# Local attention and two mixture layers on one core: six weight tiles issued from GpSimd, shared TensorE tile shapes, and a new order of passes

## The chip, the cores and the metric

One core of a Trainium2 chip runs the whole program. The metric is the device time of one execution in microseconds (us); the median of three executions of the kernel before is 485.14 us.

## What is computed

Attention over q, k and v of shape (2, 8, 576, 64) makes x; two layers follow, each a product with a 512 x 2048 matrix, a function of each element, and a product with a 2048 x 512 matrix.

```python
def _attn_ref(q, k, v):
    # q_d, k_d, v_d: means over groups of 4 positions
    out_d = sm_attn(q_d, k_d, v_d)              # coarse attention, 144 positions
    out_up = np.repeat(out_d, factor, axis=2)
    mask = np.abs(pos[:, None] - pos[None, :]) < factor
    scores = scale * np.matmul(q, k.transpose(0, 1, 3, 2))
    scores = np.where(mask, scores, -1000000000.0)
    ...
    return (out_up + out_local).astype(np.float32)

def _moe_ref(x, w_in, w_out, a, b):
    h = x @ w_in
    P = a[0] + a[1] * h + a[2] * h2 + a[3] * h3
    Q = 1.0 + np.abs(b[0]) * np.abs(h) + np.abs(b[1]) * h2
    g = P / (Q + 1e-06)
    return (g @ w_out).astype(np.float32)

def _moe2_ref(x, w_in, w_out):
    h = x @ w_in
    g = h * np.tanh(np.log1p(np.exp(h)))        # h itself where h > 20
    return (g @ w_out).astype(np.float32)
```

The weights arrive as 64-bit floats, the rest as 32-bit floats.

## The kernel before, in words

**Attention** is cut into 18 units. A unit (function `unit`) takes two heads and 256 positions (two of the 18, called mixed here, take the last 64 positions of all eight heads). Its steps are: load q (line 635); transpose it on TensorE (`flip`, line 537); write the mask into PSUM by a product with two identity matrices (line 694, `eye2` and `mask`, 64 partitions); add the local scores of 48 keys per 32 positions (line 701, output tiles of 32 columns of the array); make the coarse scores of 144 keys (line 707, one product per head, output tiles of 64 columns); softmax on VectorE, ScalarE and GpSimd (lines 719 to 762); transpose the probabilities (lines 773 and 778); multiply by v (lines 803 and 813); write the result in two parts, `xh` (rounded) and `xl` (the rest, line 857 on GpSimd). Eight times, function `prep` loads k, transposes it, copies it on ScalarE (line 578), sums groups of four on VectorE (line 588) and scales the sums (line 591).

**Weights** come in 32 tiles of 1 MB. Each is loaded by SyncE (lines 968 and 973) into one of two buffers `raw`, turned from 64-bit to 32-bit on ScalarE (lines 985 and 992) and VectorE (line 999, which frees the `raw` buffer), and split into a rounded part (line 1011) and a rest (line 1016), which together are a tile `wi` or `wo`.

**Layers.** A step of the first layer multiplies x by two column blocks of `w_in` (line 1129), reads the product from PSUM in three passes (ScalarE: square, line 1149, and absolute value, line 1152; VectorE: line 1158), forms the quotient, and multiplies by `w_out` (line 1262). From the second group of columns on, the quotient uses a logarithm and a sigmoid (lines 1084 and 1089), each with its table load (line 1073). The second layer has its own products (lines 1443, 1499 and 1264).

**Order.** No instruction is placed by hand. Class `Plan` keeps tasks with an engine, an estimated duration, a priority (smaller is earlier) and dependencies, plays them through in time, and writes each engine's instructions in the order in which they come up. Where it sees TensorE without work while little was done in the last 3.4 us, it puts in a product of zeros (line 519, called a filler here) that nothing reads. The order that results is fixed in the program: each engine works through its own list and waits where an operand is late.

Of the kernel before, what the change touches and what calls it, by code (L numbers as in the profile page):

```python
# [72 lines left out]
class Task:  # L73
    __slots__ = ("engs", "fn", "prio", "deps", "out", "next", "take", "use", "started", "ended", "seq", "dens", "port", "dma", "sub")


class Plan:
# [6 lines left out]
    def add(self, engs, fn, prio, after=(), take=(), use=(), chain=None, dens=0.5, port=False, dma=(), sub=None):  # L84
        t = Task()
        t.dma, t.sub = dma, sub
# [24 lines left out]
    def run(self, names):  # L111
# [3 lines left out]
        landed, moved = [0.0] * QUEUED, 0.0  # L115
# [75 lines left out]
        while True:  # L191
            for e in names:
# [3 lines left out]
                while ready[e]:  # L196
# [14 lines left out]
                    if e == "pool" or e == "dve" and t.port:  # L211

                        begin = max(now, port[0])
                        port[0] = begin + t.engs[e]
                    end = until[e] = begin + t.engs[e] * (2 if e == "pe" and now < COLD else 1)
                    there = end + LAT[e]
                    if t.dma:
                        end = begin
# [4 lines left out]
                        until[e], there = end, landed[-1]  # L223
# [25 lines left out]
            while events and events[0][0] <= now + 1e-9:  # L249
# [5 lines left out]
                if kind == 2:  # L255
                    del live[t.slot.space][id(t)]
                    continue
# [12 lines left out]
def kernel(  # L270
# [34 lines left out]
    eye2 = const.tile([64, 128], BF16, name="eye2")  # L305
    mask = const.tile([64, 11, WK], BF16, name="mask")
# [162 lines left out]
    def eyes():  # L469
        for h in range(2):  # L470
            nc.vector.tensor_copy(out=eye2[:, 64 * h:64 * h + 64], in_=ident[:64, :64])
# [10 lines left out]
    t_id = add({"pool": 1.1}, lambda: make_identity(nc, ident), -1000)  # L482
    t_m = add({"dve": 0.1}, lambda: nc.vector.memset(band, 0.0), -1900)
    t_cd = add({"dve": 0.6}, zeros, -1000)
# [48 lines left out]
    SCALE = 0.125  # L533
# [5 lines left out]
    def prep(bb, p, prio, slots, start):  # L539
# [36 lines left out]
        def copy(e, dst, src):  # L576
            if e == "act":
                nc.scalar.activation(out=dst(), in_=src(), func=AF.Identity)
            else:
                nc.vector.tensor_copy(out=dst(), in_=src())  # L580
# [6 lines left out]
        def red():  # L587
# [3 lines left out]
            nc.vector.tensor_scalar(out=kd[p], in0=kd[p], scalar1=SCALE / 16.0, scalar2=None, op0=ALU.mult)  # L591

        kv_done[p] = add({"dve": 0.67 + t_dve(SD, True)}, red, prio, after=copies)
# [27 lines left out]
    def unit(u, slots, start):  # L621
# [42 lines left out]
        def qcopy(e):  # L664
            dst, src = qT.v[:, :256], qp.v[:, :256]
            if e == "act":
                nc.scalar.activation(out=dst, in_=src, func=AF.Identity, scale=SCALE)
# [891 lines left out]
```

## Time and profile before

| what | value |
|---|---|
| median of three executions | 485.14 us (484.02 to 485.44) |
| the profiled execution | 484.05 us |
| its span | 482.3 us |
| TensorE clock granted | 1.00 throughout |
| TensorE, VectorE, ScalarE, GpSimd busy | 98%, 79%, 71%, 12% of the span |
| fillers in the program | 74 |

The profiled execution is 1.75 us longer than its span, which is time ahead of the first and behind the last instruction. The busy share of TensorE counts fillers as work, and the ends of its instructions are modelled; what one step costs is read from the start of one instruction to the start of the next.

### The profile page before, as it was taken

Reading aid. Unit: us, or ns where it says so; the run is one execution under the profiler, and the core shown is the slowest. Engines: PE = TensorE matmul, PEld = TensorE weight load, DVE = VectorE, ACT = ScalarE, POOL = GpSimd, SP = SyncE. Lnnn points to the kernel's source line nnn. Section 1 sums busy time; section 2 is a strip of 40 time slices with the busy share of each in tenths; the row PEclk is TensorE's granted clock in tenths of the full one; section 3 lists DMA queues with packets and bytes.
Section 4 is the critical chain, followed back from the end, with each engine's and each line's share of the span. In section 5 each row is a group of like instructions: output and inputs, shape, how many; then the busy total and the mean of one; then the engine's idle time right before and its main releaser. Section 6 shows DMA issues by size and latency. Waiting matters only on the chain.

```text
span 482.3 us, 9623 instructions
## 1 busy us (share of the span) xinstructions
PE 472.1 (98%) x3944; PEld 429.2 (89%) x3944; DVE 381.1 (79%) x569; ACT 340.6 (71%) x531; POOL 58.0 (12%) x80
## 2 busy tenths in 40 slices
PE   9989999999999999999989999999999999999996
PEld 5667788889999999999989999999989898989885
DVE  5768999989999988978999999678586769624342
ACT  5768887986889898996899987569666446422320
POOL 2664246752000000000000000000000000000000
PEclk9999999999999999999999999999999999999999
DMA  8878779620432224340412001224304220000103
GB/s 181 199 163 200 189 188 246 167 57 18 170 99 79 87 88 174 96 166 1 137 39 88 1 12 76 87 58 165 121 16 167 87 88 1 1 0 1 65 1 130
DMA packets 45980, 47.16 MB, mean 98 GB/s; under 512 B 30576, under 2 KB 31344, under 8 KB 45936
## 3 DMA queue, kind: packets, MB, share of 16 engines
q1 hardware_dynamic: 45936, 46.54, 33.9%
q8 instruction: 31, 0.51, 0.5%
q14 instruction: 13, 0.11, 0.1%
HBM read 44.17 MB, written 2.36 MB: 96 GB/s over the span
## 4 chain that ended last, share of the span: by engine, by line
PE 85%; DVE 4%; ACT 4%; DMA 4%; SPq 2%; issue 1%; POOL 0%; ACTq 0%; POOLq 0%
PE psum L1264 20%; PE psum L1262 20%; PE psum L1129 18%; PE psum L1443 12%; PE psum L1499 7%; DMA att<-in_q_dram 4%; PE psum L519 2%; PE psum L537 1%; PE psum L813 1%; PE psum L803 1%; PE psum L707 1%; PE psum L701 1%; SPq L650 1%; DVE wo L1016 1%; ACT L1073 1%
## 5 line engine op out<-in xcount | busy, mean ns | idle before, releaser
L1129 PE MATMUL psum<-xh,wi 128*128 128x384 f32 (+1 forms) x336 | 82.4, 318 | 2.0 <-ACT late_f L1152 1.8
L1262 PE MATMUL psum<-gg,wo 128*128 128x384 f32 (+1 forms) x480 | 75.9, 312 | 0.0
L1262 PEld LDWEIGHTS psum<-gg,wo 128*128 128x128 f32 x480 | 72.7, 189 | 0.6 <-issue 0.5
L1129 PEld LDWEIGHTS psum<-xh,wi 128*128 128x128 f32 x336 | 58.7, 189 | 3.7 <-ACT late_f L1152 2.1
L1129 PE MATMUL psum<-xl,wi 128*128 128x384 f32 (+1 forms) x168 | 52.4, 312 | 0.0
L1264 PE MATMUL psum<-wo,gg 128*128 128x512 f32 x216 | 51.7, 391 | 0.0
L1264 PE MATMUL psum<-wo,late_g 128*128 128x512 f32 x216 | 51.3, 391 | 0.0
L1264 PEld LDWEIGHTS psum<-wo,late_g 128*128 128x128 f32 x216 | 40.4, 188 | 8.0
L1264 PEld LDWEIGHTS psum<-wo,gg 128*128 128x128 f32 x216 | 40.4, 188 | 8.0
L999 DVE SCALAR_TENSOR_TENSOR wt<-wt,raw 128x1024 int32<-128x1024 int32 x32 | 39.8, 1248 | 6.8 <-ACT wt L985 6.6
L985 ACT ACTIVATE wt<-raw 128x1024 f32<-128x1024 f32 x32 | 36.6, 1142 | 8.1 <-DVE wo L1016 3.5
L992 ACT ACTIVATE raw<-raw 128x1024 int32<-128x1024 uint16 x32 | 36.6, 1146 | 3.9 <-DMA raw<-in_moe_w_out_dram 2.5
L1499 PE MATMUL psum<-xh,wi 128*128 128x384 f32 x128 | 34.4, 335 | 0.0
L1129 PEld LDWEIGHTS psum<-xl,wi 128*128 128x128 f32 x168 | 31.8, 189 | 0.0
L1375 DVE TENSOR_TENSOR part<-psum,part 128x512 f32<-128x512 f32 x27 | 17.8, 687 | 13.7 <-PE psum L1264 13.7
L1149 ACT ACTIVATE wrk<-psum 128x768 f32<-128x768 f32 (+1 forms) x27 | 19.8, 735 | 8.3 <-PE psum L1129 8.0
L1129 PE MATMUL psum<-xh,late_r 128*128 128x384 f32 x96 | 25.3, 334 | 0.0
L1016 DVE TENSOR_TENSOR wo<-wt,wo 128x1024 fp32r<-128x1024 f32 x14 | 17.8, 1274 | 9.4 <-ACT wo L1011 9.4
L1011 ACT ACTIVATE wo<-wt 128x1024 fp32r<-128x1024 f32 x13 | 13.8, 1061 | 16.0 <-DVE wt L1005 7.6
L1499 PEld LDWEIGHTS psum<-xh,wi 128*128 128x128 f32 x128 | 23.3, 188 | 0.2
L1073 ACT ACT_TABLE_LOAD x17 | 21.8, 1283 | 0.3
L1499 PE MATMUL psum<-xl,wi 128*128 128x384 f32 x64 | 21.4, 335 | 0.0
(164 smaller groups left out, 1044.0 us busy)
## 6 DMA issues: line engine op xcount, KB each, us to landing
raw<-in_moe_w_in_dram SPq DMA_DIRECT2D x16, 1024.0 KB, 5.3
raw<-in_moe_w_out_dram SPq DMA_DIRECT2D x16, 1024.0 KB, 5.0
att<-in_v_dram SPq DMA_DIRECT2D x64, 48.0 KB, 2.7
out_dram<-part SPq DMA_DIRECT2D x9, 256.0 KB, 2.1
att<-in_q_dram SPq DMA_DIRECT2D x16, 128.0 KB, 6.4
att<-in_k_dram SPq DMA_DIRECT2D x6, 288.0 KB, 5.3
att<-in_v_dram SPq DMA_DIRECT2D x6, 256.0 KB, 5.9
wrk<-in_k_dram SPq DMA_DIRECT2D x2, 288.0 KB
```

Of the source, the lines that this page charges most:

```text
L985: nc.scalar.activation(out=t.v, in_=words(r)[:, :, 1].bitcast(F32), func=AF.Prelu if fold else AF.Identity, scale=2.0 ** -112, **({"alpha" ...
L992: nc.scalar.activation(out=words(r)[:, :, 0], in_=r.v.bitcast(U16).rearrange("p (n four) -> p n four", four=4)[:, :, 1], func=AF.Copy, sca ...
L999: nc.vector.scalar_tensor_tensor(out=ti, in0=ti, scalar=3, in1=words(r)[:, :, 0], op0=ALU.logical_shift_left, op1=ALU.bitwise_or)
L1016: ENG[e].tensor_tensor(out=w.v[:, 1], in0=s.v, in1=w.v[:, 0].bitcast(F32), op=ALU.subtract)
L1073: nc.scalar.preload_act_table_set(name)
L1129: nc.tensor.matmul(st.h.v[:, i, :T], w.v[:, ww, ks], xx[:, kk, c0:c0 + T], start=(nn == 0 and (st.big or i == 0)), stop=(nn == 3 * KD - 1 ...
L1149: nc.scalar.activation(out=vw(st.a), in_=H(), func=AF.Square)
L1262: nc.tensor.matmul(A(d)[:, :T], w.v[:, ww, lo + d * 128:lo + (d + 1) * 128], vw(gg)[:, i, :], start=start, stop=stop)
L1264: nc.tensor.matmul(A(d), vw(gg)[:, i, sl], w.v[:, ww, lo:lo + DM], start=start, stop=stop)
L1375: nc.vector.tensor_tensor(out=pv, in0=acc.v[:, j], in1=pv, op=ALU.add)
L1443: nc.tensor.matmul(dst.v[:, :TW], wv.v[:, ww, at:at + 128], x(h, kk), start=bool(take) and nn == 0, stop=nn == 5, skip_group_check=not take,)
L1499: nc.tensor.matmul(h.v[:, i, :TW], w.v[:, ww, at:at + 128], xx[:, kk, c0:c0 + TW], start=nn == 0, stop=nn == 3 * KD - 1)
```

## The change

The six weight tiles that are needed first are issued by GpSimd, on a DMA queue of its own, and no longer by SyncE between the attention's loads. The mask product now has 128 partitions (the lower 64 are zeros), and the coarse scores are made in two pieces of 32 rows per head, in the same 64x32 tiles of the array that the local scores use. The scale of the scores moves: k is copied with 0.125/16, q with 16, so the separate scaling of the summed k is gone. The planner's model of DMA becomes one of queues that share the engines, and its priorities change: offsets per unit and per weight tile, and 15 less for the three passes that read a step's product.

```diff
-SECOND = 2.0
+SECOND = 1.6
-LEAD, CLEAD, LLEAD, OLAG = 38, 14, 40, 18
-PROL, PSTEP, VOFF, VROFF, LOFF, KOFF = -45, 3.0, 1, -1, 7, 12
+LEAD, CLEAD, LLEAD, OLAG = 38, 20, 25, 20
+PROL, PSTEP, VOFF, VROFF, LOFF, KOFF = -45, 2.5, 1, -1, 7, 12
-SUMS = 10
+SUMS = 15
+APART, PISSUE = 6, 1.2
+UOFF = [0.0, 0.0, 0.0, 0.0, 3.0, 3.0, 3.0, 3.0, 10.5, 6.0, 6.0, -1.5, 1.5, 3.0, 10.5, -4.5, 4.5, -7.5]
+GOFF = [-8.0, 0.0, 0.0, 0.0, -4.0, 0.0, -8.0, -2.0, -6.0, -4.0, 2.0, 4.0]
+HP = 15
...
+class Rings:
...
+            heads = [r[0] for r in rows.values() if r]
+            live = [j for j in heads if j[0] <= at + 1e-9]
...
+                j[1] -= (to - at) / len(live)
...
-                            end = max(end, landed[-QUEUED]) + issue
-                            moved = max(moved, end + 0.3) + move
-                            landed.append(moved + LAT["sp"])
+                            if len(lane) >= QUEUED:
+                                end = max(end, lane[-QUEUED].done + LAT["sp"])
+                            end += issue
+                            lane.append(Job())
+                            rings.put(now, e, end + 0.3, move, lane[-1])
...
-    eye2 = const.tile([64, 128], BF16, name="eye2")
-    mask = const.tile([64, 11, WK], BF16, name="mask")
+    eye2 = const.tile([128, 128], BF16, name="eye2")
+    mask = const.tile([128, 11, WK], BF16, name="mask")
...
+    def under():
+        nc.vector.memset(eye2[64:], 0.0)
+        nc.vector.memset(mask[64:], 0.0)
...
+    KSCALE = 0.125 / 16.0
+    QSCALE = 16.0
...
-                nc.scalar.activation(out=dst(), in_=src(), func=AF.Identity)
+                nc.scalar.activation(out=dst(), in_=src(), func=AF.Identity, scale=KSCALE)
...
-            nc.vector.tensor_scalar(out=kd[p], in0=kd[p], scalar1=SCALE / 16.0, scalar2=None, op0=ALU.mult)
...
-                    nc.tensor.matmul(sd2()[h], qds(i)[h], kd[p][h], start=(i == 0), stop=(p == pairs[-1]))
+                    for r0 in (h.start, h.start + HB):
+                        c0 = r0 - h.start
+                        nc.tensor.matmul(
+                            sd2()[r0:r0 + HB], qds(i)[h, c0:c0 + HB], kd[p][h], start=(i == 0), stop=(p == pairs[-1]),
+                            tile_position=(h.start, r0),
+                        )
...
-        def load(g=g, r=r):
+        def load(g=g, r=r, q=nc.gpsimd if len(W) < APART else nc.sync):
...
-        x = add({"sp": 0.5}, load, pr - LLEAD, take=[r], chain="wld", dma=[(0.5, 3.97)])
+        x = add({"pool" if len(W) < APART else "sp": 1.0}, load, pr - LLEAD, take=[r], chain="wld", dma=[(PISSUE if len(W) < APART else 0.5, 3.97)])
...
-        ta = add({"act": t_act(n, True)}, i_a, pr, after=th, take=[st.a], use=[st.h], chain="ia")
-        tb = add({"act": t_act(n, True, 1)}, i_b, pr, after=th + [t_b], take=[st.b], use=[st.h], chain="ib")
+        ta = add({"act": t_act(n, True)}, i_a, pr - HP, after=th, take=[st.a], use=[st.h], chain="ia")
+        tb = add({"act": t_act(n, True, 1)}, i_b, pr - HP, after=th + [t_b], take=[st.b], use=[st.h], chain="ib")
...
-        t1 = add({"dve": t_dve(n, ptr=1)}, d_1, pr, after=[ta, t_b], take=[st.c], use=[st.a, st.h], chain="ic")
+        t1 = add({"dve": t_dve(n, ptr=1)}, d_1, pr - HP, after=[ta, t_b], take=[st.c], use=[st.a, st.h], chain="ic")
```

In the program that comes out, lines after the first few hundred have numbers about 50 to 60 higher. Three places are shown.

GpSimd, from the mask's bands (`band`) to the first normalisation of a softmax, before:

```order
L449 AFFINE_SELECT band<-band 64x92
L452 AFFINE_SELECT band<-band 64x92
L474 MEMSET bias_69 128x1
L475 MEMSET bias_69 128x1
L607 TENSOR_TENSOR att<-att 72x4x128
L611 TENSOR_TENSOR att<-att 72x2x2x64
L757 TENSOR_TENSOR att<-att 128x4x48
L762 TENSOR_SCALAR att<-att 128x144
```

and in the change:

```order
L495 AFFINE_SELECT band<-band 64x92
L498 AFFINE_SELECT band<-band 64x92
L1026 DMA raw_74<-in_moe_w_in_dram 128x4x256
L520 MEMSET bias_69 128x1
L521 MEMSET bias_69 128x1
L1026 DMA raw_75<-in_moe_w_in_dram 128x4x256
L813 TENSOR_TENSOR att<-att 128x4x48
L818 TENSOR_SCALAR att<-att 128x144
L658 TENSOR_TENSOR att<-att 72x4x128
L813 TENSOR_TENSOR att<-att 128x4x48
L662 TENSOR_TENSOR att<-att 72x2x2x64
L1026 DMA raw_74<-in_moe_w_in_dram 128x4x256
```

Two weight loads now stand ahead of all attention work of GpSimd, and the first sum of v (L607, now L658) stands behind the first normalisation (L757, now L813).

SyncE, the loads around the first weight tile (`raw_74`), before:

```order
L601 DMA wrk<-in_v_dram 64x2x512
L601 DMA wrk<-in_v_dram 8x2x512
L968 DMA raw_74<-in_moe_w_in_dram 128x4x256
L601 DMA att<-in_v_dram 64x2x512
L601 DMA att<-in_v_dram 8x2x512
L635 DMA att<-in_q_dram 128x4x64
```

and in the change, at the same place:

```order
L652 DMA wrk<-in_v_dram 64x2x512
L652 DMA wrk<-in_v_dram 8x2x512
L686 DMA att<-in_q_dram 128x4x64
L701 DMA att<-in_v_dram 48x4x64 x4
L652 DMA att<-in_v_dram 64x2x512
L652 DMA att<-in_v_dram 8x2x512
```

No weight load stands among them; SyncE's first one comes 37 rows into its list.

ScalarE in the first layer, where the logarithm and the sigmoid of one pair of steps stand (each behind its table load) and the passes that read the next product, before:

```order
L1073 ACT_TABLE_LOAD
L1084 ACTIVATE wrk<-wrk,bias_69 128x768
L1084 ACTIVATE late_f<-late_f,bias_69 128x768
L1149 ACTIVATE wrk<-psum 128x768
L1073 ACT_TABLE_LOAD
L1089 ACTIVATE wrk<-wrk 128x768
L1089 ACTIVATE late_f<-late_f 128x768
L1152 ACTIVATE late_f<-psum,b_sb 128x768
```

and in the change:

```order
L1131 ACT_TABLE_LOAD
L1142 ACTIVATE wrk<-wrk,bias_69 128x768
L1142 ACTIVATE late_f<-late_f,bias_69 128x768
L1043 ACTIVATE wt_77<-raw_75 128x1024
L1207 ACTIVATE wrk<-psum 128x768
L1210 ACTIVATE late_f<-psum,b_sb 128x768
L1131 ACT_TABLE_LOAD
L1147 ACTIVATE wrk<-wrk 128x768
L1147 ACTIVATE late_f<-late_f 128x768
```

The second pass over the product (L1152, now L1210) stands directly behind the first, ahead of the second table load.

On TensorE the program has 111 fillers where it had 74, and otherwise as many products of each shape as before, but for the coarse scores (96 of 32 rows for 48 of 64). Ahead of the local scores of the first, third, sixth and ninth unit stand 24, 61, 96 and 110 fillers where there were 20, 35, 50 and 59; behind those of the ninth stood 15, and now stands one. Of the first layer's first products 36 stood ahead of the ninth unit's local scores, and now 51.

## Rows read from the trace of the kernel before

**Rows 1.** The page's part 1: engine, busy us, share of the span, instructions.

```profile
PE 472.1 (98%) x3944; PEld 429.2 (89%) x3944; DVE 381.1 (79%) x569; ACT 340.6 (71%) x531; POOL 58.0 (12%) x80
```

**Rows 2.** Waits of TensorE in the whole span: us in total, times, longest.

```profile
PE psum L537 <- DMA att<-in_q_dram: 2.7, 3, 1.5
PE psum L1129 <- ACT late_f L1152: 1.8, 1, 1.8
PE psum L1129 <- DVE wi L1016: 0.2, 1, 0.2
PE psum L537 <- ACT att L788: 0.2, 1, 0.2
```

**Rows 3.** Timeline of TensorE: start us, us, instruction, count.

```profile
13.68 1.38 PE L519 MATMUL psum<-blank 128*128 128x480 bf16 x6
14.89 0.38 PE L773 MATMUL psum<-ident,att 128*112 128x128 f32 x2
...
33.89 0.28 PE L1129 MATMUL psum<-xl,wi 128*128 128x256 f32 x1
34.01 0.28 PE L1129 MATMUL psum<-xh,wi 128*128 128x256 f32 x1
34.22 0.25 PE L694 MATMUL psum<-mask,eye 64*128 64x192 bf16 x1
...
34.40 0.54 PE L701 MATMUL psum<-att 64*32 64x48 f32 x32
34.88 0.46 PE L707 MATMUL psum<-att 64*64 64x144 f32 x4
35.27 0.39 PE L1129 MATMUL psum<-xh,wi 128*128 128x256 f32 x1
...
46.63 1.20 PE L707 MATMUL psum<-att 64*64 64x144 f32 x16
47.76 0.69 PE L537 MATMUL psum<-ident,att 96*128 96x96 f32 x5
```

**Rows 4.** Timeline of SyncE's queue: start us, us of the issue.

```profile
17.62 0.40 SPq L968 DMA_DIRECT2D raw<-in_moe_w_in_dram  x1
...
19.37 1.01 SPq L635 DMA_DIRECT2D att<-in_q_dram  x1
```

**Rows 5.** The chain that ended last, at 19 us: start us, us.

```profile
19.37 8.48 DMA att<-in_q_dram
```

**Rows 6.** The page's part 6: issues, KB each, median us to landing.

```profile
raw<-in_moe_w_in_dram SPq DMA_DIRECT2D x16, 1024.0 KB, 5.3
```

**Rows 7.** Windows: us, busy us of PE, PEld, DVE, ACT, POOL, PEclk, DMA share, GB/s.

```profile
5.00:10.00 5.00, 5.00 (x65) 3.32 (x64) 1.75 (x4) 3.60 (x9) 0.13 (x1) 1.00 1.12 222
15.00:20.00 5.00, 4.95 (x109) 3.15 (x111) 3.69 (x12) 3.47 (x13) 2.84 (x5) 1.00 0.66 150
...
50.00:60.00 10.00, 9.19 (x162) 7.17 (x161) 9.60 (x19) 8.15 (x22) 3.53 (x5) 1.00 0.68 187
```

**Rows 8.** Timeline of GpSimd: start us, us.

```profile
14.63 0.39 POOL L762 TENSOR_SCALAR att<-att 128x144 f32<-128x144 f32 x1
14.98 1.27 POOL L607 TENSOR_TENSOR wrk<-wrk 72x512 f32<-72x512 f32 x1
...
41.23 1.36 POOL L762 TENSOR_SCALAR att<-att 128x144 f32<-128x144 f32 x1
```

**Rows 9.** Timeline of VectorE: start us, us.

```profile
8.84 0.23 DVE L591 TENSOR_SCALAR att<-att 128x144 f32<-128x144 f32 x1
...
40.99 1.33 DVE L1016 TENSOR_TENSOR wi<-wt,wi 128x1024 fp32r<-128x1024 f32 x1 [0.43 <-ACT wi L1011]
```

**Rows 10.** Timeline of ScalarE at 240 us: start us, us.

```profile
240.79 0.79 ACT L1149 ACTIVATE wrk<-psum 128x768 f32<-128x768 f32 x1
241.59 1.28 ACT L1073 ACT_TABLE_LOAD   x1
...
244.37 0.88 ACT L1152 ACTIVATE late_f<-psum,b_sb 128x768 f32<-128x768 f32 x1
```

More of the change, by code (lines that the diff above doesn't have):

```diff
@@ L73, with __init__, step, put @@
 class Task:
-    __slots__ = ("engs", "fn", "prio", "deps", "out", "next", "take", "use", "started", "ended", "seq", "dens", "port", "dma", "sub")
+    __slots__ = ("engs", "fn", "prio", "deps", "out", "next", "take", "use", "started", "ended", "seq", "dens", "port", "dma", "sub", "job")
+class Rings:
+    def __init__(self):
+        self.at, self.rows = 0.0, {}
+    def step(self, rows, at, until):
+        while True:
+            heads = [r[0] for r in rows.values() if r]
+            live = [j for j in heads if j[0] <= at + 1e-9]
+            ends = [j[0] for j in heads if j[0] > at + 1e-9] + [at + j[1] * len(live) for j in live]
+            if not ends or at >= until:
+                return at
+            to = min(min(ends), until)
+            for j in live:
+                j[1] -= (to - at) / len(live)
+            at = to
+            for r in rows.values():
+                if r and r[0][0] <= at + 1e-9 and r[0][1] <= 1e-9:
+                    r[0][2].done = at
+                    r.popleft()
+    def put(self, now, row, begin, move, job):
+        self.step(self.rows, self.at, now)
+        self.at = max(self.at, now)
+        self.rows.setdefault(row, deque()).append([begin, move, job])
+        self.step({k: deque([list(j) for j in r]) for k, r in self.rows.items()}, self.at, 1e9)
+class Job:
+    done = 0.0
 class Plan:
@@ L210, in run @@
                     begin = max(now, 0.65) if e == "sp" else now
-                    if e == "pool" or e == "dve" and t.port:
+                    if e == "pool" and not t.dma or e == "dve" and t.port:
                         begin = max(now, port[0])
@@ L217, in run @@
                     if t.dma:
-                        end = begin
+                        end, lane = begin, lanes["soft" if e == "pool" else "sp"]
                         for issue, move in t.dma:
-                            end = max(end, landed[-QUEUED]) + issue
-                            moved = max(moved, end + 0.3) + move
-                            landed.append(moved + LAT["sp"])
-                        until[e], there = end, landed[-1]
+                            if len(lane) >= QUEUED:
[3 more added lines that the diff above has]
+                            rings.put(now, e, end + 0.3, move, lane[-1])
+                        t.job = lane[-1]
+                        until[e], there = end, t.job.done + LAT["sp"]
                     n += 1
@@ L256, in run @@
                     del live[t.slot.space][id(t)]
+                    continue
+                if t.job is not None and t.job.done + LAT["sp"] > now + 1e-6:
+                    n += 1
+                    heapq.heappush(events, (t.job.done + LAT["sp"], n, 1, e, t))
                     continue
@@ L666, in qcopy @@
             if e == "act":
[L667 removed]
+                nc.scalar.activation(out=dst, in_=src, func=AF.Identity, scale=QSCALE)
             else:
[L669 removed]
+                nc.vector.tensor_scalar(out=dst, in0=src, scalar1=QSCALE, scalar2=None, op0=ALU.mult)
         def qsum():
@@ L926 @@
     need[3].append((1, 2, 0))
[L927 removed]
+    att_last, att_order = [], []
     seen = set()
```

26 lines of the change are left out of this document (13 added, 13 removed).

## The prediction

> **What bounds the kernel now.** I read the page first: TensorE is busy in 98% of the span [rows 1], so the end moves only if its list of instructions gets shorter or waits less. The view of waits then says what it waits for: 2.7 us in three waits of a q transpose for the load of q, 1.8 us once for the second ScalarE pass over a product, and two of 0.2 us [rows 2]. That is small, because the planner filled the longer gaps itself: 74 of the products are fillers, and TensorE's timeline shows what one takes: six begin at 13.68 and the next instruction at 14.89, so 0.202 us each [rows 3]. Fillers stand in the list for good; a filler costs its time whether the data came early or late. So the account of this change is one of TensorE: fillers more or fewer, shorter steps, waits gone and waits new. The other engines count only where they make TensorE wait. The last view is the DMA share by windows: 1.12 between 5 and 10 us, 0.66 between 15 and 20 us [rows 7], so the DMA engines are full in the first part of the attention and not behind it.
>
> **The change part by part.**
>
> *Fillers.* The program has 111 for 74. 37 x 0.202 us [rows 3] = **7.5 us more**: 110 stand ahead of the ninth unit's local scores where there were 59, and one behind where there were 15. They are there because the new plan sends two weight tiles (2 MB) into the start and expects q and k later. Nothing hides them, since TensorE has no gap to put them in.
>
> *Mask and coarse scores.* Between two products of the layers lie 0.12 us (33.89 to 34.01), from such a product to the mask 0.21 us (34.01 to 34.22) [rows 3]. Changing from the full array to 64 rows costs 0.09 us, and the new mask is of the full array. In the new order 14 of 18 mask products follow a product or transpose of the full array, four follow the products with v: 14 x 0.09 = 1.3 us less. The coarse scores of a plain unit take 0.39 us for 4 instructions (34.88 to 35.27), those of a mixed one 1.13 us for 16 (46.63 to 47.76) [rows 3]: 12 more instructions in 0.74 us, so 0.247 us for four, and 0.143 us is left for entering and leaving that shape. Half of one change and half of the next make one whole change, and one whole change goes: 18 x 0.143 = 2.6 us. The bound on the other side: the local scores, already in the new shape, run 32 instructions of 48 columns in 0.48 us (34.40 to 34.88) [rows 3], 0.31 ns for a column; eight pieces of 144 columns would take 0.36 us, only 0.03 us less than now, 18 x 0.03 = 0.5 us. I take 2.6, since it comes from the coarse scores themselves, and keep 0.5. Together **3.9 us less** (1.8 at the low end).
>
> *q waits.* Before, SyncE issues a weight tile at 17.62 and a q load at 19.37 [rows 4]; that q load takes 8.48 us until TensorE can go on [rows 5], while a weight tile needs a median of 5.3 us to land [rows 6]. In the new order no weight load stands between SyncE's attention loads, and q has no tile ahead of it in its queue. I take all **2.7 us** [rows 2] as gone; the other end is that they stay. The Trainium skill, "DMA: Bandwidth & Descriptors", section "Issuing engines are not separate DMA queues", says against this that DMAs run on the same engines whoever issues them and that several issuers save issue time only. By that rule the 2.7 us stay and the sum below would be +1.8 us. The trace of before has one queue and cannot show it.
>
> *Passes that read a product.* At 240 us ScalarE runs the first pass (240.79), a table load of 1.28 us (241.59), two sigmoids, and only at 244.37 the second pass [rows 10], which frees the product's place in PSUM; TensorE's 1.8 us wait [rows 2] is for that. In the new order the second pass stands directly behind the first, ahead of the table load. **1.8 us less**; late next are the two sigmoids, which move back by one pass (0.88 us [rows 10]) and have a plan of other steps between them and TensorE.
>
> *GpSimd's issues.* Six of them, and what one takes is not in this trace: between 0.40 us (SyncE's issue of the same tile [rows 4]) and 1.27 us (GpSimd's sum of v [rows 8]), 2.4 to 7.6 us in all on an engine that is busy 12% of the span [rows 1]. Two stand before all attention work. Behind each of the other four wait sums of v and normalisations, and a unit's probabilities behind those. I take nothing for TensorE, because the fillers already stand for the later units; it is a rival below. SyncE loses six issues of 0.40 us; that is part of the q term.
>
> *Scaling of k.* Eight VectorE passes of 0.23 us go [rows 9], and two memsets come in the first microseconds. Taken at nothing: TensorE's list there consists of fillers whichever comes first.
>
> *Sum.* 7.5 - 3.9 - 2.7 - 1.8 = -0.9 us. The profiled execution took 484.05 us (span 482.3 and 1.75 around it), so 483.15 on its scale. The median of the runs is 485.14, 1.09 above it: **484.2 us**. The term for the scores at its low end makes it 2.1 us more. A measurement of this kernel can tell about 0.3%, 1.45 us, from no change, and the forecast lies inside that.
>
> **Rivals.**
>
> *Faster: the early tiles unload VectorE.* Between 50 and 60 us VectorE is busy 9.60 of 10 us, between 15 and 20 us 3.69 of 5 [rows 7]. Three tiles are now unpacked ahead of 30 us; each costs VectorE at least its last pass, 1.33 us [rows 9], and, as an estimate, as much for the joining pass before it, some 2.6 us, so 8 us of VectorE leave the full stretch. If a quarter of that held TensorE in holds too short for the view of waits, 2 us more go: -2.9 us, 482.2. For it: the new order has 51 first-layer products ahead of the ninth unit's local scores, where there were 36. Against it: the named waits on VectorE come to 0.2 us [rows 2].
>
> *Slower: the DMA engines are shared.* Two tiles go out at about 2 us and take at least 2 x 5.3 = 10.6 us of landing [rows 6], where the engines are full already (1.12, [rows 7]). The new order allows for it with 26 more fillers ahead of the third unit (61 for 35), 5.3 us. What the tiles cost beyond that is new waits of TensorE for q and k: at most 5.3 us, less what fits where the engines had room (0.66). It decides from the point at which q and k of the third and fourth unit land later than their places in TensorE's list, around 20 and 25 us. Then the q waits also stay (+2.7). With the waits alone +1.8 us, with 2.65 more +4.5; I set it at +3.1, 488.2.
>
> *Slower: GpSimd's issues are held.* GpSimd's scaling of 144 columns took 0.39 us at 14.63 and 1.36 us at 41.23, where VectorE's 1.33 us pass with two inputs ran from 40.99 [rows 8, 9]: held 0.97 us. An issue so held delays the normalisations queued behind it on GpSimd by 1.27 + 0.97 = 2.2 us. Were one of the four on TensorE's path, -0.9 + 2.2 = +1.3 us, 486.4; two, +3.5. The Trainium skill, "SBUF — State Buffer", section "SBUF: two separate sides", states the same for issuing: GpSimd cannot write its DMA descriptors while VectorE holds the port they share. That it happens to a DMA no run here shows yet.
>
> *It does not do what it says.* Only two `raw` buffers exist, so the third to sixth tile can start only when an earlier tile is joined; only two of six loads are free to be early. This is inside the forecast.
>
> **How the numbers follow.** Forecast 0.46, faster rival 0.21, shared engines 0.20, held issues 0.13. The forecast's own spread, -2.5 to +1.2 us, gives 0.17 to faster and 0.29 to same. The faster rival gives 0.20 and 0.01, shared engines 0.02 to same and 0.18 to slower, held issues 0.05 to same and 0.08 to slower. Together 0.37, 0.37 and 0.26. The range reaches from a little below the faster rival to the shared engines' time: 481.5 to 488.5; the forecast's own is 482.6 to 486.3.
>
> **What would show it.** Right: 111 fillers of 0.202 us; no wait of TensorE for q over 1 us and none for the second pass at 240 us; from the coarse scores to the next instruction at most 0.3 us; tail as before. Wrong: TensorE waiting for q or k between 10 and 30 us (shared engines), GpSimd's normalisations coming late behind a weight issue (held issues), coarse scores still at 0.39 us (shapes), or ScalarE waiting at its first weight pass for a tile, with k copies queued behind it.

## The result, and the profile after

The changed kernel takes 488.5 us (median of six runs, 487.35 to 490.07), the kernel before 484.07 us in the same comparison: a ratio of 1.0099, 95% interval 1.0071 to 1.0126. It is **slower by 4.4 us**. The prediction was 484.2 us, and no change that could be told; 488.5 is the upper end of its range. TensorE's mean granted clock is not the same in every run, and runs at 0.998 or more have a median of 488.0 us after (three runs) and 482.9 before (51 runs of all comparisons): the difference there is 5.0 us.

The two profiled executions are 3.3 us apart (span 485.6 us for 482.3): the one after is the fastest of its six runs, and the one before is 1.1 us above the 482.9, so the traces can account for 3.3 us and not for all of the difference. The page's part 1 of the kernel after, beside [rows 1]:

```profile
PE 475.8 (98%) x4077; PEld 431.9 (89%) x4077; DVE 380.5 (78%) x565; ACT 339.0 (70%) x529; POOL 63.5 (13%) x86
```

TensorE is busy 3.7 us longer, and the rest of its span (485.6 - 475.8 for 482.3 - 472.1) is 0.4 us shorter: 3.7 - 0.4 = 3.3. VectorE and ScalarE are busy about as long as before; GpSimd has its six issues more. The waits of TensorE after (line, what it waits for, us, times, longest), beside [rows 2]:

```profile
PE psum L589 <- DMA att<-in_q_dram: 1.4, 1, 1.4
PE psum L570 <- DVE band L533: 1.2, 1, 1.2
PE psum L752 <- ACT att L718: 0.7, 1, 0.7
PE psum L1501 <- DVE wrk L1523: 0.7, 1, 0.7
PE psum L760 <- issue: 0.5, 1, 0.5
PE psum L869 <- issue: 0.4, 1, 0.4
PE psum L1187 <- POOL xl L913: 0.3, 1, 0.3
PE psum L834 <- POOL att L818: 0.3, 1, 0.3
PE psum L745 <- ACT att L791: 0.2, 1, 0.2
```

The wait for `band`, ahead of the first filler, is as long before (1.2 us). Of the others, the 1.8 us wait for the second pass at 240 us [rows 2] is gone and the q waits are down from 2.7 to 1.4, but seven small waits of 3.1 us in all have come: together 4.5 us, where [rows 2] has 4.9. The new shapes are in TensorE's timeline after (start, us):

```profile
9.27 0.57 PE L570 MATMUL psum<-blank 128*128 128x480 bf16 x2
9.68 0.25 PE L745 MATMUL psum<-mask,eye 128*128 128x192 bf16 x1
9.85 0.55 PE L752 MATMUL psum<-att 64*32 64x48 f32 x32
10.22 0.43 PE L760 MATMUL psum<-att 64*32 64x144 f32 x8
10.58 0.58 PE L570 MATMUL psum<-blank 128*128 128x480 bf16 x2
```

From the coarse scores to the next instruction it is 0.36 us (10.22 to 10.58), not the 0.25 I had taken, but the local scores before them now end after 0.37 us instead of 0.48: together the 0.14 us per unit of the forecast's term, in another place (0.36 is the price that the prediction's other bound gave for the coarse scores).

The whole difference can be added up on TensorE, counting each instruction from its start to the next start, with the waits that the profile names taken out. From before to after the fillers take 7.0 us more, the local scores 2.0 less, the coarse scores 0.4 less, and the masks, transposes and products 0.9 less: 3.7 us, for 3.6 in the forecast (7.5 - 3.9). The waits take 0.4 us less, for 4.5 in the forecast (2.7 + 1.8). So TensorE's list came out as predicted, and its waits did not.

**Where it went.** Each unit has one mask product, so the mask's starts date the units. TensorE's timelines, the second and the sixth unit of the kernel before:

```profile
11.04 0.25 PE L694 MATMUL psum<-mask,eye 64*128 64x192 bf16 x1
...
30.12 0.25 PE L694 MATMUL psum<-mask,eye 64*128 64x192 bf16 x1
```

and after, with the last products with v of the whole attention:

```profile
16.41 0.25 PE L745 MATMUL psum<-mask,eye 128*128 128x192 bf16 x1
...
41.88 0.25 PE L745 MATMUL psum<-mask,eye 128*128 128x192 bf16 x1
...
123.96 0.67 PE L869 MATMUL psum<-att 48*64 48x32 f32 x32
```

The units are 5.4 us late at the second and 11.8 us at the sixth; the last products with v begin at 123.96 us where they began at 116.90:

```profile
116.90 0.67 PE L813 MATMUL psum<-att 48*64 48x32 f32 x32
```

More layer work has been done between the units by then, so the net is less: counting TensorE's instructions for the layers' products in the traces, the 400th stands at 136.6 us for 132.1, **4.5 us late**. About 2.1 us come back at 240 us, where the wait is gone, and 0.9 us is lost again between 310 and 316 us, in the second layer, where TensorE waits 0.7 us for VectorE (L1501): 4.5 - 2.1 + 0.9 = 3.3, the difference of the spans. So the loss of the traced execution is the attention's.

What stands at its start is two weight tiles. GpSimd's timeline after:

```profile
1.87 0.98 POOL L1026 DMA_DIRECT2D raw<-in_moe_w_in_dram  x1
2.92 0.76 POOL L1026 DMA_DIRECT2D raw<-in_moe_w_in_dram  x1
```

They land at 9.61 and 14.77 us. SyncE's queue in the same stretch (start, us of the issue):

```profile
3.29 0.64 SPq L597 DMA_DIRECT2D wrk<-in_k_dram  x1
3.97 1.96 SPq L652 DMA_DIRECT2D att<-in_v_dram  x2
5.97 0.61 SPq L686 DMA_DIRECT2D att<-in_q_dram  x1
6.63 2.43 SPq L597 DMA_DIRECT2D wrk<-in_k_dram  x1
9.10 1.15 SPq L652 DMA_DIRECT2D wrk<-in_v_dram  x2
13.94 0.61 SPq L686 DMA_DIRECT2D att<-in_q_dram  x1
```

The third load of k, issued at 3.29, lands at 15.51 us, and an issue that takes 0.6 us elsewhere takes 2.43. And TensorE's order allows for it: 17 fillers stand between the scores of the first and the second unit, where 3 stood.

### The profile page after: what moved, and what is told of

It is laid out like the page before. It is cut to its first block, busy times and chain, and to the rows that moved or that the text cites. A ratio compares the mean times of both kernels' runs of the same rounds, so it can differ in the third digit from the quotient of the medians.

```text
span 485.6 us, 9881 instructions
## 1 busy us (share of the span) xinstructions
PE 475.8 (98%) x4077; PEld 431.9 (89%) x4077; DVE 380.5 (78%) x565; ACT 339.0 (70%) x529; POOL 63.5 (13%) x86
## 4 chain that ended last, share of the span: by engine, by line
PE 78%; DVE 11%; ACT 4%; DMA 3%; issue 1%; POOL 1%; SPq 0%; ACTq 0%; POOLq 0%
PE psum L1187 19%; PE psum L1322 18%; PE psum L1320 16%; PE psum L1501 11%; PE psum L1557 5%; DMA att<-in_q_dram 2%; PE psum L869 2%; DVE wi L1074 2%; PE psum L859 1%; PE psum L752 1%; PE psum L570 1%; PE psum L589 1%; PE psum L760 1%; DVE wt L1057 1%; PE psum L829 1%
## 5 line engine op out<-in xcount | busy, mean ns | idle before, releaser
L1187 PE MATMUL psum<-xh,wi 128*128 128x384 f32 (+1 forms) x336 | 83.7, 320 | 0.0
L570 PE MATMUL psum<-blank 128*128 128x480 bf16 x111 | 28.6, 394 | 1.2 <-DVE band L533 1.2
L1069 ACT ACTIVATE wo<-wt 128x1024 fp32r<-128x1024 f32 x11 | 11.7, 1059 | 18.9 <-DVE wt L1063 7.7
```

Of the source, the lines that this page charges most:

```text
L570: nc.tensor.matmul(view[:, :480], blank[:, :128], blank, start=True, stop=True)
L1187: nc.tensor.matmul(st.h.v[:, i, :T], w.v[:, ww, ks], xx[:, kk, c0:c0 + T], start=(nn == 0 and (st.big or i == 0)), stop=(nn == 3 * KD - 1 ...
```

## The experiments

Each ratio is to runs of the kernel before on the same chip; its median there was 483.1 to 484.3 us.

### Which part: the shapes, the order of the passes

**Shapes alone** (kernel before, all orders kept):

```diff
-    mask = const.tile([64, 11, WK], BF16, name="mask")
+    mask = const.tile([128, 11, WK], BF16, name="mask")
...
+                    for r0 in (h.start, h.start + HB):
```

> The kernel before with the new shapes alone (mask and identity of 128 partitions, coarse scores in two pieces of 32 rows per head), the planned durations left as they were, so that every engine's order is that of before. Theory: TensorE's list is the bound, and the shapes shorten it by the 3.9 us of the prediction (0.145 us in 18 units and 0.09 us in 13 or 14), so 3 to 4 us (0.6 to 0.8%) less than before. Rival: the later steps of a unit wait for VectorE and ScalarE anyway, and TensorE only waits where it was shorter: under 1 us less.

Measured: 484.2 us, ratio 1.0018 [0.9993, 1.0042]. Nothing gained. In its trace TensorE is 1.5 us ahead of before at the 400th product and up to 240 us: 2.4 us have left its list by then, not 3.9, and 0.9 us of new waits has come. Then it waits the same 1.8 us for ScalarE, and this happens (windows: us, busy us of PE, PEld, DVE, ACT, POOL, granted clock, DMA share, GB/s):

```profile
242.00:244.00 2.00, 0.23 (x2) 0.20 (x2) 1.91 (x3) 2.00 (x4) 0.00 (x0) 1.00 0.00 0
244.00:246.00 2.00, 2.00 (x8) 2.00 (x8) 1.93 (x3) 2.00 (x4) 0.00 (x0) 0.59 0.00 0
246.00:248.00 2.00, 2.00 (x8) 2.00 (x8) 2.00 (x4) 2.00 (x3) 0.00 (x0) 0.56 0.00 0
```

After a window in which TensorE worked 0.23 of 2 us, its granted clock stands for most of 4 us at the lower of its two levels (1.2 GHz for 2.4): 2 x (0.41 + 0.44) = 1.7 us of work, the whole lead. The kernel before had the same wait, and kept its clock.

**Shapes and the lead of the passes** (`HP = 15` as in the change, 82 fillers):

> The kernel before with the new shapes and with 15 less for the priorities of the three passes that read a product; weights still from SyncE, planner otherwise as before (82 fillers for 74). Theory: the wait of 1.8 us for the second pass at 240 us goes, eight fillers more cost 1.6 us, the shapes give 3.9: 4 us (0.8%) less than before. Rival: passes moved ahead delay others, and new waits behind 235 us take the 1.8 us back: 2 us less than before at most.

Measured: 487.6 us, ratio 1.0092 [1.0058, 1.0125]. The wait at 240 us went, as expected, and 3.4 us were lost against the shapes alone. In its trace 1.7 us go with a clock of 0.50 and 0.66 from 54 to 58 us, behind a q wait of 1.4 us, 1.0 in a wait for VectorE at 195 us, and some 2 where the layers meet (TensorE waits 1.1 us for VectorE and 0.6 for ScalarE between 300 and 332 us). The fall of the clock is not the reason: its four runs at a clock of 0.999 or more have a median of 487.3 us.

**The lead taken out of the change** (`HP = 0`, all else kept):

> The changed kernel with the product-reading passes' lead taken back (from 15 us to 0), all else kept. Theory A, that this lead is the loss (3.4 us more in the kernel before with the shapes): the time is 484.0 to 485.5 us, the end of the attention comes 2 to 3 us earlier than with the change, and the wait of 1.8 us for ScalarE's second pass near 240 us is back. Theory B, that the loss is made in the first 30 us, by the weight tiles that arrive there and by the spread steps: the end of the attention stays 4 us behind before, and with the wait at 240 us back the time is 488.5 to 490.5 us.

Measured: 491.67 us, ratio 1.0181 [1.0156, 1.0206]: in the changed orders the same lead gains 3.2 us. It is not the loss, and the parts do not add.

**The lead for two steps only**, those at 240 us, with the shapes (`pr - (HP if idx in (21, 22) else 0)`):

> The kernel before with the shared shapes, and the product-reading passes put first for two steps of the first layer alone, those whose passes stand at 235 to 245 us on ScalarE (indices 21 and 22). TensorE, ScalarE and VectorE have the same order as with the shapes alone up to that place. With the shapes alone TensorE was 1.5 us ahead of before at 240 us, waited 1.8 us there for ScalarE's second pass, and ran 4 us at a granted clock of 0.56 to 0.59 after it, which took the 1.5 us back. Theory A, that this wait and the low clock behind it are what kept the shapes' gain from the end: the wait goes, no stretch of low clock stands at 244 to 248 us, and the time is 480.5 to 482.0 us (1.8 + 1.5 less than the 484.2 of the shapes alone, or a little less than that). Theory B, that ScalarE is full there (1.97 to 2.00 us of every 2 us between 236 and 258) and the passes that give way come late to someone else: the wait at 240 us is gone, another of about 2 us stands between 245 and 270 us, and the time is 483.5 to 484.5 us.

Measured: 483.9 us, ratio 1.0014 [0.9998, 1.003]; theory B by the time, though its wait of 2 us behind 245 us did not come. The wait is gone and the 1100th layer product stands at 251.6 us (252.9 before), but where the two layers meet (1380th product) it is 303.3 for 303.4: between 296 and 302 us VectorE is busy 6.00 of 6.00 us, and TensorE waits 0.8 us there for gate values. Its trace had lost the shapes' 1.5 us before that, at a low clock from 53 to 58 us behind a q wait of 1.9 us; its seven runs at a clock of 0.998 or more have a median of 483.8 us, so that is not what hides a gain.

### The fillers, the early loads, the queue

**37 fillers fewer** (the change, with 74 fillers emitted, its order otherwise kept):

```diff
-                    fns[-1](s.view)
+                    given[0] += 1
+                    k = given[0] - 13
+                    if k <= 0 or k * 61 // 98 > (k - 1) * 61 // 98:
+                        fns[-1](s.view)
```

> The changed kernel with the same plan and order, but 37 of its 111 fillers not written (spread over the 98 behind the first 13), so 74 as before. Theory A (a filler costs its own time): 37 x 0.202 = 7.5 us less than the changed kernel, 481 us. Theory B (a filler stands where data comes late anyway): TensorE waits in their place, its waits grow by about what the fillers took, and the time is that of the changed kernel within 2 us, 486.5 to 488.5 us, as long as the clock stays granted.

Measured: 488.4 us, ratio 1.0104 [1.0051, 1.0158]. Nothing gained; waits took the fillers' place:

```profile
PE psum L756 <- ACT att L722: 3.3, 3, 1.6
PE psum L593 <- DMA att<-in_q_dram: 3.1, 1, 3.1
```

Against the change, TensorE's fillers take 7.1 us less, its waits 6.1 us more. But this is not a clean price of fillers:

```profile
12.00:14.00 2.00, 0.00 (x0) 0.00 (x0) 0.00 (x0) 0.94 (x3) 0.00 (x0) 0.84 1.10 218
14.00:16.00 2.00, 1.60 (x5) 0.86 (x6) 0.84 (x3) 0.41 (x2) 0.00 (x0) 0.50 1.17 179
16.00:18.00 2.00, 2.00 (x10) 0.61 (x8) 0.84 (x3) 2.00 (x2) 1.58 (x3) 0.50 1.11 201
```

Without them TensorE stood still and then ran at the lower clock, which took 2.9 us more; none of the four runs was granted the full clock (0.993 to 0.996).

**All weights issued by SyncE** in the changed planner (`APART = 0`, 121 fillers):

> The changed kernel with all weight tiles issued by SyncE (the number of tiles on GpSimd's queue set to 0), all else of the change kept; the planner then gives 121 fillers. Theory: the loss comes from 2 MB of weights in the first 15 us beside the attention's loads; with SyncE they start later, the first units come earlier, but q loads stand behind tiles again; near the changed kernel, 486 to 490 us, with waits for q over 2 us. Rival: GpSimd's queue is the whole loss: 484 us or less.

Measured: 492.33 us, ratio 1.0169 [1.0105, 1.0233]. The second unit stands at 10.6 us again, but the first layer product at 44.0 us (35.3 in the change, 33.7 before); `LLEAD` is 25 in this planner for 40 before. In the changed numbers the queue is worth 4 us, and it is not the loss. It also says that late tiles alone do not make a good order: what the planner does with them can cost more than the tiles.

**The two early tiles moved behind the fourth k load and the second v load**, issued by SyncE, all orders of TensorE, ScalarE and VectorE kept:

```diff
+            load()
+            if gone[0] == 4:
+                late_w.pop(0)(q=nc.sync)
```

> The changed kernel with the first two weight tiles issued by SyncE behind the fourth k load and the second v load instead of by GpSimd at 1.9 and 2.9 us; every other order is that of the change. Theory A, that these 2 MB hold back the first k and q loads and so cost the attention: the third k load lands before 12 us instead of at 15.5, the waits of TensorE and VectorE before 25 us shrink, the attention ends 2 to 4 us earlier and the time is 484.5 to 486.5 us. Theory B, that the order itself (the units spread over more fillers) sets the pace and the loads only fill it: k lands earlier, the time stays within 1 us of 488.5 us, or grows by 1 to 3 us where ScalarE's first weight pass now waits for its tile.

Measured: 488.17 us, ratio 1.0108 [1.0077, 1.0138]; theory B. The third k load landed at 9.25 us instead of 15.51 and the second unit came at 14.05, but the third came at 23.98 (22.56 in the change), because TensorE now waits 1.9 us for ScalarE behind its weight passes, and then ran at the lower clock from 19 to 23 us (1.7 us of work). The clock does not decide it: the three runs at 0.998 or more have a median of 487.5 us, for 488.0 in the change. Earlier data hardly help an order that was written for late data.

**The changed planner with the old numbers** (no offsets, no lead, 120 fillers):

> The first six weight tiles issued by GpSimd in the changed planner, with the shared shapes, but with the planner's numbers of before (leads, steps, no offsets for units or tiles) and no lead for the product-reading passes; 120 fillers. Against the shapes alone (484.2 us) it has only the queue's change and what the planner makes of it. Theory A, that GpSimd's queue is harmless or better: 483.0 to 485.0 us. Theory B, that 2 MB of weights in the first 15 us delay k and q, whatever the numbers: 486.5 to 489.0 us, with the third unit's scores after 20 us (before: 16.0 us).

Measured: 496.2 us, ratio 1.025 [1.0219, 1.028]. Theory B in direction, and worse: second unit at 19.0 us, sixth at 47.5. So the changed numbers (4.5 us) and the lead (3.2 us) repair 7.7 of the 12 us that the early tiles and the new model of DMA, which come together here, cost with the old ones. Some of the 12 is the clock: none of its runs was granted more than 0.997, and its trace lost 3.4 us of work to the lower level.

**The queue alone** (kernel before, six tiles issued by GpSimd at the same places):

```diff
-                nc.sync.dma_start(
+                q.dma_start(
```

> The kernel before, with the first six weight tiles issued by GpSimd at the places in time at which its planner has SyncE issue them; the orders of TensorE, VectorE and ScalarE are those of before, word for word. So the queue alone. Theory A, that a queue of its own takes the tile out of q's way: TensorE's q waits (2.7 us before) fall below 1 us, no stretch of low clock follows them, and the time is 481.5 to 483.5 us. Theory B, that the engines behind the queues are shared and q waits just as long, or that an issue on GpSimd (0.75 to 0.98 us with the change) delays its normalisations: 484 to 486 us, with q waits of 2 us or more.

Measured: 484.14 us, ratio 1.0004 [0.998, 1.0028]. Its waits of TensorE:

```profile
PE psum L1129 <- ACT late_f L1152: 1.8, 1, 1.8
PE psum L778 <- POOL att L762: 1.3, 2, 1.0
PE psum L519 <- DVE band L483: 1.2, 1, 1.2
PE psum L813 <- DMA att<-in_v_dram: 0.7, 1, 0.7
PE psum L803 <- DVE att L833: 0.7, 2, 0.4
```

The q waits are gone, as in theory A, and the time is theory B's: waits of 1.3 us for GpSimd's normalisations, 0.7 for v and 0.7 for VectorE stand there instead, which before had not [rows 2]. **The queue, the shapes and the scale in the copies**, in the orders of before:

> The same queue alone, with the shared shapes and the scale moved into the copies of k and q: every part of the change but its planner's numbers, its DMA model and the lead of the product-reading passes, in the orders of before. Theory A, that these parts are harmless or better and the loss is all in the orders: 480.0 to 483.0 us. Theory B, that two queues or the issues on GpSimd cost something whatever the orders are: 484.5 us or more.

Measured: 485.36 us, ratio 1.0037 [1.0015, 1.0059], between the theories. A q wait of 1.8 us is there at 28 us, a v wait of 1.0 at 33, and the lower clock from 34 to 38 us and again from 246 to 250 (1.7 us of work each time). What is left of the 4.4 us must lie in the orders, the early place of the two tiles among them.

**The cause: the early tiles together with the orders that allow for them.** The change, with one dependency more, which the planner and the chip both see:

```diff
-load, pr - LLEAD, take=[r], chain="wld", ...
+load, pr - LLEAD, after=k_loads[3:4] if len(W) < 2 else [], take=[r], chain="wld", ...
```

> The changed kernel with the first two weight loads told to wait, in the planner and on the chip, for the fourth k load (they are still issued by GpSimd); everything else of the change is kept, and the planner writes the orders anew: 25, 35, 37 and 48 fillers stand ahead of the second to fifth unit's scores, nearly as before (23, 35, 37, 43), where the change has 41, 61, 72 and 85; 100 fillers in all. Theory A, that the loss is the place of these two tiles, in the loads and in the orders that allow for them (moving the loads alone gave nothing, and fewer fillers alone gave nothing): the second unit's scores stand before 12 us and the sixth's before 34 us (16.4 and 41.9 with the change, 11.0 and 30.1 before), the attention ends 3 to 5 us earlier, and the time is 483.5 to 486.0 us. Theory B, that the other numbers of the planner or the lead of the product-reading passes make the loss: the units come early, the end of the attention stays within 1.5 us of the change's, and the time is 487 to 490 us.

Measured: **484.16 us**, ratio 1.0013 [0.9992, 1.0035], wholly below the change's interval. TensorE's timeline, second and sixth unit:

```profile
11.68 0.24 PE L747 MATMUL psum<-mask,eye 128*128 128x192 bf16 x1
...
30.98 0.25 PE L747 MATMUL psum<-mask,eye 128*128 128x192 bf16 x1
```

The third k load lands at 8.48 us, the weights leave at 14.85 and 20.27 us. The 400th layer product stands at 130.2 us: 6.4 us ahead of the change and 1.9 ahead of before. The last products with v end only 1.7 us earlier than with the change, less than the 3 to 5 expected. With the two tiles out of the way, and every other part of the change kept, the loss is gone: it lies in those two tiles' place, in the loads and in the order around them together, since moving the loads alone gave nothing. What this does not exclude is that another order for early tiles would have done as well: each such run is one order that the planner found, and its orders differ by several us (492.33 us without early tiles, above). One more order with the tiles behind k, at the end of these experiments and with 18 VectorE instructions fewer, took 484.04 us.

It is no proof that fillers cost nothing. Against before, 26 more fillers take 5.4 us of TensorE's list, the changed shapes and what goes with them give back 4.4, and the waits 1.1: before's time, by a sum.

### Where gains go

The lead of 1.9 us was gone again at 337 us: the trace has five fillers at 225 us and waits of 0.9 us for VectorE behind them, and a wait of 1.0 us for VectorE at 310 us, against the 2.1 us that come back at 240. I tried VectorE's list as the bound of the first layer. **More VectorE work** (one sum of the softmax made three times from the ninth unit on):

```diff
+            for _ in range(3 if summed[0] > 8 else 1):
```

> The kernel before, in which the sum over 48 keys of the softmax (VectorE, 0.35 us) is made three times instead of once in the ninth to the eighteenth unit: 20 more VectorE instructions, 6.9 us, between 50 and 110 us; the orders of all other engines are those of before. Theory A, that VectorE's list sets the end of the first layer (in every trace so far the time of the first layer's end is 264 to 277 us plus the time in which VectorE had been idle until then: 275.0 + 27.7 before, 269.3 + 35.8 with the change): the time grows by 4.5 to 7 us, to 488 to 490.5 us, and nearly all of it stands at the end of the attention (132.2 us before). Theory B, that TensorE's list sets it (named waits on VectorE were 0.2 us in all) and VectorE has room in its 21% of idle time: 483.5 to 485.0 us.

Measured: 486.66 us, ratio 1.0065 [1.0045, 1.0085]. Between the theories: VectorE's work until the 400th product rises by 5.1 us, and that product comes 2.1 us later.

**Less VectorE work**, the scale in the copies alone (eight passes gone), and in a second kernel also the 18 additions of 1e-9:

```diff
-            nc.vector.tensor_scalar(out=kd[p], in0=kd[p], scalar1=SCALE / 16.0, scalar2=None, op0=ALU.mult)
...
-            nc.vector.reciprocal(out=tm.v[:, 10:15], in_=tm.v[:, 10:15])
+            nc.vector.reciprocal(out=tm.v[:, 10:15], in_=tm.v[:, 5:10])
```

> The kernel before with one more part of the change alone: the scale moves into the copies of k and q, and the eight passes over the summed k (3.3 us of VectorE in all, four of them in the first 20 us) are gone; the orders are those of before. Theory A (VectorE sets the end of the first layer): 1 to 2.5 us less, 481.0 to 482.5 us. Theory B (TensorE's list does): 483.0 to 484.5 us.

> The kernel before without the eight passes over the summed k and without the 18 additions of 1e-9 to the sums of the softmax (5.7 us of VectorE, 0.32 us each; the sums are at least 1, where 1e-9 is below the last bit of a 32-bit float): 9.0 us less of VectorE, the orders otherwise those of before. Theory A: 3.5 to 7 us less, 476.5 to 480.0 us, with VectorE's idle time until the end of the first layer about as before (27 to 30 us) and that end before 299 us. Theory B: 483.0 to 484.5 us, the idle time of VectorE 8 to 9 us longer.

Measured: 483.11 us, ratio 0.9987 [0.997, 1.0004], and 483.8 us, ratio 1.0001 [0.9976, 1.0026]: theory B both times. In the second, TensorE waited 2.3 us for q, and then:

```profile
26.00:28.00 2.00, 0.20 (x2) 0.00 (x0) 0.00 (x0) 0.72 (x1) 0.05 (x1) 1.00 0.25 59
28.00:30.00 2.00, 1.53 (x14) 0.94 (x14) 0.61 (x2) 2.00 (x6) 1.92 (x2) 0.93 0.47 109
30.00:32.00 2.00, 2.00 (x67) 1.65 (x67) 1.64 (x4) 1.20 (x6) 0.26 (x2) 0.50 0.62 100
...
38.00:40.00 2.00, 2.00 (x40) 1.24 (x38) 1.14 (x4) 2.00 (x7) 1.12 (x2) 0.51 0.39 89
```

10 us at half clock, 5 us of work. **The same in the change** (18 additions gone), and **in the kernel with the tiles behind k**:

> The changed kernel without the 18 additions of 1e-9 (VectorE, 5.1 us), the orders otherwise those of the change. Theory A, that VectorE is the bound here too, and the loss of the change is VectorE's idle time (22.6 us until the end of the attention, 16.7 before): 2 to 4.5 us less than the 488.4 us of the change, 484.0 to 486.5 us. Theory B, that TensorE's fillers and late loads set the pace of the units: 487.5 to 488.5 us.

> The kernel with the two early loads behind the fourth k load, without the 18 additions of 1e-9 to the sums of the softmax (5.1 us of VectorE; the sums are at least 1), the orders otherwise the same. With the loads moved the kernel is 1.9 us ahead of before at 190 us and level with it at 337 us; VectorE has no gap between 297 and 312 us, and TensorE waits 1.0 us for it there. Theory A, that what is won in the attention is lost because VectorE is behind when the layers meet: VectorE's idle time until then grows by less than 3 us, the wait of 1.0 us goes, and the time is 481.0 to 483.0 us. Theory B, that VectorE's place in the second layer is set by orders and not by its backlog: the time is 483.5 to 485.0 us.

Measured: 487.74 us, ratio 1.0093 [1.0057, 1.013], and 483.66 us, ratio 1.0019 [0.9993, 1.0045]. Both theories B, by the time. In the first a q wait grew from 1.4 to 3.3 us and the 400th product stayed (137.0). In the second the profile is 1.5 us ahead of before from 337 us to the end, span 480.7 us; the runs do not bear it out. Nine of them at a clock of 0.998 or more have a median of 483.4 us, and ten such runs of the kernel before, in the same comparison, 482.0. **The last four steps without the lead**, on top:

> The same, and the lead of the product-reading passes kept for the steps up to the second of the last group (indices 0 to 22) and taken back for the last four steps of the first layer, which end where VectorE is full. Theory A, that this lead pushes VectorE's and ScalarE's other passes into the place where the layers meet: 0.5 to 1.5 us less than without that, 480 to 482.5 us. Theory B, that it does nothing there: within 0.5 us of it.

Measured: 484.04 us, ratio 1.0016 [0.9995, 1.0037]: nothing. No version beat the kernel before. Of all these, VectorE work added costs a third to a half of itself (2.4 us for 6.9; at full clock 3.2); VectorE work removed brings nothing that can be measured.

## Why the prediction was wrong

The forecast was -0.9 us on the profile's scale, the measured difference +3.3 there and +4.4 in the medians.

- **The step that failed: the waits.** The forecast took 4.5 us of waits as gone (2.7 for q, 1.8 for the second pass) and put the new ones at nothing ("I take all 2.7 us", "I take nothing for TensorE"). Of TensorE's waits 4.9 us stood before and 4.5 after: 1.3 of the q waits and the 1.8 went, and 3.1 us came in seven small waits, for ScalarE, VectorE, GpSimd and in places where the profile names no cause. That is 4.1 of the 4.2 us between forecast and trace.
- **Base.** "The end moves only if its list of instructions gets shorter or waits less" holds in the traces: 3.7 - 0.4 = 3.3. What it hides is that list and waits trade against each other: where 37 fillers were left out, 6.1 of their 7.1 us came back as waits.
- **Fillers, +7.5 us.** Their number was right (111), and their price nearly so (7.0 us; two that begin at 9.27 are followed at 9.68). "Nothing hides them" is right as a sum and wrong as a cause: most of them stand where the unit's data are not there, and they were the mark of what did cost, a plan that sends two tiles ahead of k and q.
- **Shapes, -3.9 us.** 3.3 us less in the trace, with everything but fillers and waits counted; with the shapes alone 2.4, of which 1.5 reached 240 us and nothing the end. That the whole list came within 0.1 us of the forecast is partly luck, since this term and the fillers' are off by about as much and the other way.
- **q waits, -2.7 us.** 1.3 us went in the change. With the queue alone all went, and the time stayed, since other waits came. The Trainium skill, "DMA: Bandwidth & Descriptors", section "Issuing engines are not separate DMA queues", holds that issuers save only issue time because the transfers share the same engines. The 15.51 us landing of k beside two tiles from another queue agrees with it, and so does the time of the queue alone; that its q waits vanished does not.
- **Passes, -1.8 us.** The wait went as predicted and 2.1 us came back at that place. "Two sigmoids late next" was not the price; 0.9 us was lost early in the second layer, with a wait of 0.7 us for VectorE.
- **What would show it.** Of the signs of being right, 111 fillers and the missing wait at 240 us came true; a q wait of 1.4 us (at most 1 was named) and 0.36 us from the coarse scores to the next instruction (at most 0.3) did not.
- **Rivals.** "DMA engines are shared" gave 488.2 us and named the two tiles and the third and fourth unit. Place and sign were right, and its size too, in part by luck: 1.4 us of the q waits stayed, and new waits came, but few of them are for q or k and most stand behind 30 us. The late data themselves had been written into the order as fillers, which the sum already held. "Early tiles unload VectorE" did not show: the layers' 400th product is 4.5 us later. "GpSimd's issues are held": they took 0.75 to 0.98 us, none was long, and the one wait of 1.38 us was for a `raw` buffer; as a rival it shows only in the queue-alone run's 1.3 us.

Open: why the runs at full clock are 5.0 us apart and the traced executions 3.3; no trace of a faster execution of the kernel before is there. Open too is whether early tiles must cost, or only in the order that was found for them.

## What to carry to other kernels

A busy share that contains fillers does not say what the engine would do without them: here 6.1 of 7.1 us of fillers left out came back as waits. Count list and waits together, do not take a wait as gone without asking what ends next at that place, and date the stages by a mark that occurs once per unit. A load that is made earlier goes ahead of something; look at what is needed first, and at whether the order was written around its arrival, since then neither moving the load nor dropping the padding alone helped here. Parts of a change that pass through a planner do not add: the same lead cost 3.4 us in one order and gained 3.2 in another.

## What was not expected of the hardware

A single wait of TensorE of about 2 us can cost as much again, or more, and no rule for when it does comes out of these runs. Of the eighteen waits of 1.8 to 3.5 us in the nineteen profiles told of here, nine were followed at once by the lower level of the granted clock (0.59 and 0.56 after the wait at 240 us; 0.50 for 10 us after one of 2.3 us at 27 us) and nine were not, among them one of 3.3 us at 15 us. The same wait of 1.8 us near 240 to 260 us was followed by it in four kernels (the shapes alone, the scale in the copies, the fewer additions, the queue with the shapes) and not in five (before, the queue alone, more VectorE work, the change without the lead, the old numbers). The clock also fell four times, ahead of the kernels' last microseconds, behind waits of 1.4 us and less. Each fall took 1.7 us of work or more, up to 5.1. In the profile of the change, with 111 fillers, the clock was granted in full until the last microsecond; with 74 of them it stood at 0.50 from 14 to 20 us.
